# Linear attention then a GELU MLP on one Trainium2 core: counts made on VectorE and TensorE instead of GpSimd, a shorter row of idle products, and new orders for the periods

## The chip, the cores and the metric

The kernel runs on one core of a Trainium2 chip. A core has a matrix engine (TensorE; PE in the profile, its weight loads PEld), a vector engine (VectorE, DVE), an activation engine (ScalarE, ACT), a general engine (GpSimd, POOL) and SyncE (SP). Each works through its own list of instructions in order, and they wait for each other by semaphores. Sixteen DMA engines move data between device memory and the core's own memory; here POOL's queue issues all loads and converts float32 to bfloat16 on the way, and SP's queue issues the stores and some transposes. Products land in PSUM; the kernel names eight banks of it: `uY`, `uV`, `uZ`, `mY`, `mR`, `a0`, `a1`, `a2`.

The metric is the device time of one execution in microseconds (us). The kernel before has a median of 207.54 us over three runs (207.53 to 207.77).

## What is computed

Decayed linear attention over 4 sequences of 768 positions with 8 heads of 64, then an MLP with exact GELU over the 3072 resulting rows:

```python
for b in range(nb):                       # blocks of the sequence
    intra = (qb @ kb.T * Dmask) @ vb      # Dmask[i, j] = lam ** (i - j) for i >= j, else 0
    inter = (qb * lam_pow) @ kv_state
    out[:, :, sl] = intra + inter
    kv_state = lam_block * kv_state + (kb * rev_pow).T @ vb
x = out.transpose(0, 2, 1, 3).reshape(3072, 512)
h = x @ w_in                              # 512 -> 2048
y = gelu(h) @ w_out                       # 2048 -> 512, float32 out
```

The kernel takes blocks of 128 positions where the reference takes 64; the decay makes the two the same.

## The kernel before, in words

The 768 positions are cut into six groups (`NG = 6`) of 128 positions for all four sequences, that is, 512 rows a group. Group g's attention gives `xs[g]`, then the first MLP product with GELU gives `gts[g]`, then the second product gives the output rows. The stages overlap: while group g is in its first MLP product, group g-1 is in its second one and group g+1 in attention. TensorE's list is written out by hand, as strings of letters that are worked off one after the other, and the place of a letter sets the place of its instructions on every engine's list.

**The head** (`HEAD`, L727). POOL issues the loads in the order of `LOADS1`, behind the first load of k (L129) and of q (L132). `load(0, 0, ..)` is half a group, two DMAs. Between the two loads POOL writes two iotas (L130, L131): `pos`, the number of the partition, and `row`, the counts 0 to 127 along the free axis. From them VectorE makes the identity `ident` for the transposes and the thresholds `posp`, `negj` and masks `cmask_p`; ScalarE makes powers of lam (`lam_mp`, `lam_q`). In `HEAD`, "." is one idle product (`keep_warm`, L740), 128 x 512 on zeros, whose result nobody reads; K and Q are transposes of k and q (`p_transposes`, L340), S scores and their masks (`p_scores`), O attention outputs (`p_outputs`, L389, then `p_x` L404), m and n parts of the first MLP product (`mm1_part`), z state products. Two of the masks `m_p` are made by POOL (L186), between its loads.

**Groups 0 and 1** (`PHASE1`, L819; `PHASE2`, L838): p is a part of group 0's second product, i, w and t make sums of weights on VectorE (`sums_w_in`, `sums_w_out`), k, q, s, o, h are steps of attention.

**The periods** (loop at L873, g = 2 to 5). Both MLP products use Strassen's scheme in Winograd's form, seven products for eight. The first product of group g is cut into four units, each with seven products p1 to p7 (`unit_slots`, L545); one product is four matmuls of 256 columns, a *slot*. A unit works in three PSUM banks: p5 fills `uV`, which ScalarE copies to `Vs` in SBUF (L586); p1 fills `uY`; ScalarE copies `uY` over `uV` (the *seed*, L578); then p2 adds to `uV`, which becomes block X, and p6 may add to `uY`. After p6 VectorE adds `uY` and `Vs` into `uZ` (L606), after p7 into `Vs` (L615); p3 adds to `uZ`, p4 to `uY`. GELUs on ScalarE (L568) empty the four blocks, and the bank of a block can be written again after its GELU. So there are four short chains between slots: p1, seed, p6; p6, add, p7; p7, add, p4; p4, GELU, p1 of the next unit. The second product of group g-1 has 28 slots of the same size (`mm2_slots`, L632). The strings `PA` (g = 2), `PB` (3 and 4) and `PC` (5) interleave them: a is the next slot of the units (order 1 5 6 2 7 3 4 in the first unit, 5 1 6 2 7 3 4 in the others), m the next slot of the second product, v a visit of attention for group g+1 (`front` and `outputs`), h a scaling of v on ScalarE, x a sum of x on VectorE, Y a decay of the state, c a DMA transpose, K, Q, V loads. `LA`, `LB` and `LC` give lags: how many slots later an add or a mask goes on VectorE's list. Attention of the last group is done in period 4, so in period 5 its PSUM banks (`a0`, `a1`, `a2`) are free until the second product of group 5 takes `a0` and `a1`.

After the periods the second product of group 5 runs alone.

Of the kernel before, what the change touches and what calls it, by code (L numbers as in the profile page):

```python
# [8 lines left out]
F32 = mybir.dt.float32  # L9
BF16 = mybir.dt.bfloat16  # L10
ALU = mybir.AluOpType
# [4 lines left out]
def kernel(  # L16
# [11 lines left out]
    B, H, S, D = q.shape  # L28
    d_model, d_ff = moe_w_in.shape
    C = 128  # L30
    NG = S // C
# [32 lines left out]
    def later(n, fn):  # L64
        later_no[0] += 1
        later_list.append((slot_no[0] + n, later_no[0], fn))
# [21 lines left out]
    def load(g, pair, name):  # L88
        if pair == 0:
            raw[g, name] = raw_pool.tile([128, B, H, D], BF16, tag="r" + name, name="raw_" + name, bufs=1 if name == "q" else 2)  # L90
        t = raw[g, name].rearrange("p (n a) h d -> p n (a h d)", n=2)[:, pair].rearrange("p (h t d) -> p h t d", h=H, t=2)
        for b in range(2):
            G.dma_start(t[b * 64:(b + 1) * 64].rearrange("p h t d -> p h (t d)"),
                        dram[name][2 * pair + b, :, g * C:(g + 1) * C, :].rearrange("h (p t) d -> p h (t d)", t=2))
        raw[g, pair, name] = t
# [17 lines left out]
    s_in = [w_pool.tile([128, 2, d_ff // 2], BF16, name=f"s_in{i}") for i in range(4)]  # L113
# [13 lines left out]
    pos = consts.tile([128, 1], F32)  # L127
    row = consts.tile([128, C], F32)
    load(0, 0, "k")  # L129
    G.iota(pos, pattern=[[0, 1]], base=0, channel_multiplier=1, allow_small_or_imprecise_dtypes=True)  # L130
    G.iota(row, pattern=[[1, C]], base=0, channel_multiplier=0, allow_small_or_imprecise_dtypes=True)  # L131
    load(0, 0, "q")  # L132


    idle = consts.tile([128, 256], BF16)
    V.memset(idle, 0.0)  # L136
    ident = consts.tile([128, 128], BF16)
    cmask = consts.tile([128, 2, C], F32)
    cmask_p = consts.tile([128, 2, 2, 64], F32)
# [20 lines left out]
    for hi in range(2):  # L160
        p = slice(hi * D, (hi + 1) * D)
# [383 lines left out]
    def unit_slots(g, u, lags):  # L545

        x = xs[g].rearrange("p k s c -> p k (s c)")
        lo, hi = 2 * u * 128, 1024 + 2 * u * 128
        st = {}
        t = gts[g]  # L550
        bl, bh = slice(2 * u, 2 * u + 2), slice(8 + 2 * u, 10 + 2 * u)

        def prod(dst, w, f0, x_of, start):
            for b in range(2):
                for ko in range(2):
                    P.matmul(dst[:, b, :], w(ko, f0 + b * 128), x_of(ko),  # L556
                             start=(start and b == 0 and ko == 0), stop=True, skip_group_check=True)

        wl = lambda ko, f: w_in_t[:, ko, f:f + 128]
        wh = lambda ko, f: w_in_t[:, 2 + ko, f:f + 128]  # L560
        ws = lambda i: (lambda ko, f: s_in[i - 1][:, ko, f:f + 128])
        x11 = lambda ko: x[:, ko, 0:256]
        x21 = lambda ko: x[:, 2 + ko, 0:256]
        x22 = lambda ko: x[:, 2 + ko, 256:512]
        tx = lambda i: (lambda ko: t_x[g][i - 1][:, ko, :])

        def gelu(name, dst, src):
            A.activation(dst, src, ACT.Gelu)  # L568
            done.add(("g", g, u, name))
            if name in "ZW" and ("g", g, u, "Z") in done and ("g", g, u, "W") in done:  # L570
                later(lags["S"][0], lambda: sums_g(g, u, 1))
            if all(("g", g, u, n) in done for n in "XYZW"):
                for n, i in enumerate((2, 4, 3)):
                    later(lags["S"][1 + n], lambda i=i: sums_g(g, u, i))

        def seed():
            if "V" in st and "Y" in st:
                A.copy(st["V"], st["Y"])  # L578
                done.add(("seed", g, u))

        def p5():
            need(("tx", g, 1))
            st["V"] = bank("uV", [128, 2, 256])
            prod(st["V"], ws(1), lo, tx(1), True)
            st["Vs"] = work.tile([128, 2, 256], F32, tag="Vs", name="Vs")
            A.copy(st["Vs"], st["V"])  # L586
            seed()

        def p1():
            need(("x", g, 0), ("x", g, 1))  # L590
            st["Y"] = bank("uY", [128, 2, 256])
            prod(st["Y"], wl, lo, x11, True)
            seed()

        def p2():
            need(("seed", g, u))
            prod(st["V"], wh, lo, x21, False)
            gelu("X", t[:, bl, 0:256], st["V"])

        def p6():  # L600
            need(("seed", g, u), ("tx", g, 2))
            prod(st["Y"], ws(2), lo, tx(2), False)

            def z():
                st["Z"] = bank("uZ", [128, 2, 256])
                V.tensor_add(st["Z"], st["Y"], st["Vs"])  # L606
                done.add(("Z", g, u))
            later(lags["Z"], z)

        def p7():  # L610
            need(("Z", g, u), ("tx", g, 3))
            prod(st["Y"], ws(3), lo, tx(3), False)

            def w():
                V.tensor_add(st["Vs"], st["Y"], st["Vs"])  # L615
                done.add(("W", g, u))
                gelu("W", t[:, bh, 256:512], st["Vs"])
            later(lags["W"], w)

        def p3():  # L620
            need(("Z", g, u))
            prod(st["Z"], ws(4), lo, x22, False)
            gelu("Z", t[:, bl, 256:512], st["Z"])

        def p4():
            need(("W", g, u), ("tx", g, 4))
            prod(st["Y"], wh, hi, tx(4), False)
            gelu("Y", t[:, bh, 0:256], st["Y"])

        return [p5, p1, p6, p2, p7, p3, p4]  # L630

    def mm2_slots(g, lags):  # L632
# [91 lines left out]


    LOADS1 = "Q1 i0 V0 K1 m1 i4 m0 V1 i2 i1 i5 s0 i3 w0 s1 i7 i6 k0 q0 w1 w4 w2 w5 k1 q1 v0 v1 w3 w6 w7"
    HEAD = "b . . . . . . . . . . . . . K M M . . . . Q d . . . . S S Q . . . . . . . . . O . . . . K . . S . S m . . . g O m n z n n n m m m n m m n m n n"  # L727

    def script(text, actions):
        for word in text.split():  # L730
            fn = actions[word]
            (fn.pop(0) if isinstance(fn, list) else fn)()

    tags = ["uY", "uV", "uZ"]
    idle_ps = {}

    def idle_bank(tag):
        idle_ps[0] = bank(tag, [128, 2, 256], F32, "idle_ps")

    def keep_warm():  # L740
        P.matmul(idle_ps[0], idle[:, :128], idle[:, None, :].to_broadcast((128, 2, 256)), start=True, stop=True)  # L741

    part_no = [0]

    def mm1_part(g, i, pair, lag=None):
# [22 lines left out]
    for item in LOADS1.split():  # L768
        i = int(item[1:])
# [8 lines left out]
        else:  # L778
            load(int(item[0].islower()), i, item[0].lower())
    script(HEAD, {  # L780
        ".": keep_warm,
        "g": lambda: (need("lam_q"), A.activation(warm, pos, ACT.Gelu)),
        "d": decays,
        "M": [lambda x=x: mask_p(0, x, V) for x in range(2)],
        "b": lambda: idle_bank("uZ"),
        "K": [lambda i=i: p_transposes(0, i, "k", "mY", ((A, A), (V, A))[i]) for i in range(2)],
        "Q": [lambda i=i: p_transposes(0, i, "q", "mR", ((V, A), (A, A))[i]) for i in range(2)],
        "S": [lambda i=i: p_scores(0, i // 2, i % 2, (("a0", "a1"), ("uY", "uV"), ("a0", "a1"), ("mY", "mR"))[i]) for i in range(4)],
# [27 lines left out]
        "z": lambda: p_state_products(1, ("a0", "a1")),  # L816
        "y": lambda: decay(2, raw["tmp", 1]),
    }
    PHASE1 = "i i i w k q i p p p w p s k q p p p t s p p w t h s h o w p p p p s p p o p"  # L819
    script(PHASE1, attn_1)  # L820


# [12 lines left out]
    new_gs(1)  # L835
    new_x(2)
    L2S = "2393225802261242"
    PHASE2 = "q z m k y n s q m n h s k n V m K s o n m n t s h m t Q c n c o Z x c M x m m c n m x x n"  # L838

    def digits(text, i, n):  # L840
        return [int(c) for c in text[i * n:(i + 1) * n]]

    script(PHASE2, {
        "m": [lambda i=i: mm1_part(1, i, 0, L2S) for i in (0, 4, 1, 5, 2, 6, 3, 7)],
# [19 lines left out]

    PA = "mKaammmahmQvhYaaamaahYmamYhhmmaYhhhmmaavammcamVmcaacvmammmaavcaaamavmaammaxaxxmmamxm"
    PB = "hQaKahhhhvmhmhhmVamvmaamamamamammaammacvacamamamccmavamammamavamamxmaamaaxxmammx"
    PC = "aammmmamamamaammaammamaammaaamammamaaammaamammaammamamma"
    LA = "2211100002302032034341221002332000000020022"  # L870
    LB = "2010000142522221213032570306003201000104020"
    LC = "0000011000112251125020230133113202105202242"
    for g in range(2, NG):  # L873
        seqs, lag = {2: (PA, LA), 5: (PC, LC)}.get(g, (PB, LB))
        LZ, LW, LS, LM, LV = lag[0:4], lag[4:8], lag[8:24], lag[24:28], lag[28:43]
# [16 lines left out]
        for c in seqs:  # L892
# [6 lines left out]
            elif c == "v":  # L899
                i = visits.pop(0)  # L900
# [5 lines left out]
            elif c == "c":  # L906
                x = cross.pop(0)
                if g + 2 < NG:
                    crossbar(g + 2, *x)
            elif c == "h":  # L910
                h = heads.pop(0)
                if att:
                    scale_v_group(g + 1, h)
            elif c == "x":
                i = sums.pop(0)
# [41 lines left out]
```

## Time and profile before

| | |
|---|---|
| runs | 207.54 us (207.53 to 207.77), three runs |
| the profiled execution | 206.72 us, of which its span is 204.6 us |
| TensorE busy | 198.7 us, 97% of the span |
| VectorE, ScalarE, GpSimd busy | 145.7, 121.4, 71.2 us |
| idle products | 40, 12.8 us |
| moved by DMA | 23.48 MB in the packets traced |

Times inside the trace count from the start of the span. A row of the timeline gives start, duration, engine, line, operation, what it writes and reads, shape and count; behind it in brackets, the idle time of its engine before it and what ended it. A row of the chain (of work that ended last) gives start, duration, engine, tile and line, and how many instructions were merged. "Busy" of TensorE is modelled: matmuls are pipelined, so a matmul counts as busy from its issue to its modelled end, and short waits between two matmuls show not as idle time but as longer groups in the chain.

### The profile page before, as it was taken

How to read it: one execution, taken by the hardware profiler on the slowest of the kernel's cores; microseconds unless marked ns; L12 is line 12 of the kernel's file. 1: busy time of each engine (PE TensorE's matmuls, PEld its weight loads, DVE VectorE, ACT ScalarE, POOL GpSimd, SP SyncE). 2: the span in 40 equal slices, each digit the busy share in tenths (PEclk: the TensorE clock that was granted, in tenths of full speed). 3: DMA queues.
4: the chain of work that ended last, by engine and by line, in shares of the span. 5: the costliest groups of instructions: out<-in, count | busy, mean ns of one | idle time of the engine just before them, and what ended most of it. 6: DMA issues, size and time to landing. Idle time of an engine off the chain costs nothing.

```text
span 204.6 us, 6259 instructions
## 1 busy us (share of the span) xinstructions
PE 198.7 (97%) x2648; PEld 156.1 (76%) x2648; DVE 145.7 (71%) x315; ACT 121.4 (59%) x248; POOL 71.2 (35%) x97
## 2 busy tenths in 40 slices
PE   7998999999999999999999999999999999999993
PEld 2454788545578888888878888888888888888882
DVE  3477482859657899699989599797699655765243
ACT  5445466283479857973588753788555566654310
POOL 7999977866493099100077100000000000000000
PEclk9999999999999999999999999999999999999999
DMA  5999999999999999994729997230002030011214
GB/s 54 141 181 180 188 182 198 183 195 181 239 160 152 125 138 119 145 99 104 157 53 157 147 144 145 83 103 3 0 3 94 13 103 3 0 51 60 97 54 155
DMA packets 81580, 23.48 MB, mean 115 GB/s; under 512 B 69776, under 2 KB 81040, under 8 KB 81552
## 3 DMA queue, kind: packets, MB, share of 16 engines
q0 software_dynamic: 62704, 13.64, 80.1%
q1 hardware_dynamic: 18848, 9.44, 19.7%
q8 instruction: 21, 0.34, 0.7%
q14 instruction: 7, 0.06, 0.1%
HBM read 27.27 MB, written 6.29 MB: 164 GB/s over the span
## 4 chain that ended last, share of the span: by engine, by line
PE 94%; DVE 3%; ACT 1%; issue 0%
PE p_uY L556 14%; PE p_mY L718 14%; PE p_mR L718 9%; PE p_uV L556 7%; PE idle_ps L741 6%; PE p_a L718 5%; PE p_uY L755 5%; PE p_uV L755 5%; PE p_uZ L755 4%; PE p_uZ L556 3%; PE t_ps L346 3%; PE p_mY L535 2%; PE p_uY L535 2%; PE p_uZ L535 2%; PE p_uV L535 2%; PE p_a L300 2%
## 5 line engine op out<-in xcount | busy, mean ns | idle before, releaser
L718 PEld LDWEIGHTS <-g_t 128*128 128x128 bf16 x304 | 29.5, 98 | 3.7
L556 PEld LDWEIGHTS <-s_in 128*128 128x128 bf16 x256 | 24.4, 97 | 5.0 <-issue 1.6
L755 PEld LDWEIGHTS <-w_in_t 128*128 128x128 bf16 x256 | 24.2, 98 | 4.8 <-issue 1.4
L718 PEld LDWEIGHTS <-gs 128*128 128x128 bf16 x240 | 23.2, 98 | 2.9
L556 PEld LDWEIGHTS <-w_in_t 128*128 128x128 bf16 x192 | 18.5, 97 | 2.9
L568 ACT ACTIVATE g_t<-p_uV 128x512 bf16<-128x512 f32 x16 | 9.5, 596 | 18.0 <-PE p_uV L556 18.0
L556 PE MATMUL p_uY<-tx,s_in 128*128 128x256 bf16 x128 | 19.2, 272 | 0.3 <-DVE p_uZ L606 0.3
L386 DVE TENSOR_TENSOR sc_m<-p_a,m_p 128x512 bf16<-128x512 f32 x20 | 12.9, 686 | 8.1 <-PE p_a L379 8.1
L606 DVE TENSOR_TENSOR p_uZ<-p_uY,Vs 128x512 f32<-128x512 f32 x16 | 11.2, 697 | 8.7 <-PE p_uY L556 8.4
L718 PE MATMUL p_mY<-w_out_t,g_t 128*128 128x256 bf16 x128 | 16.9, 273 | 0.0
L568 ACT ACTIVATE g_t<-Vs 128x512 bf16<-128x512 f32 x16 | 10.1, 630 | 10.4 <-DVE Vs L615 10.4
L615 DVE TENSOR_TENSOR Vs<-p_uY,Vs 128x512 f32<-128x512 f32 x16 | 11.0, 688 | 5.4 <-PE p_uY L556 5.1
L741 PE MATMUL idle_ps<-idle 128*128 128x512 bf16 x40 | 12.8, 463 | 1.1 <-DVE idle L136 1.1
L505 DVE TENSOR_TENSOR gs<-g_t 128x512 bf16<-128x512 bf16 x20 | 8.4, 420 | 6.4 <-ACT g_t L568 6.3
L755 PE MATMUL p_uV<-x_t,w_in_t 128*128 128x256 bf16 x88 | 11.6, 273 | 1.2 <-DVE x_t L408 1.2
L108 POOL DMA_DIRECT2D raw_v<-in_v_dram x12 | 9.9, 859 | 7.9 <-ACT o_sb L541 4.5
L100 POOL DMA_DIRECT2D raw_q<-in_q_dram x3 | 5.2, 1736 | 20.9 <-DMA qT<-raw_q 20.9
L586 ACT COPY Vs<-p_uV 128x512 f32<-128x512 f32 x16 | 9.4, 591 | 4.0 <-PE p_uV L556 4.0
L755 PE MATMUL p_uY<-x_t,w_in_t 128*128 128x256 bf16 x88 | 11.4, 273 | 0.0
L535 PEld LDWEIGHTS <-g_t 128*128 128x128 bf16 x64 | 5.7, 97 | 6.7
L578 ACT COPY p_uV<-p_uY 128x512 f32<-128x512 f32 x16 | 9.2, 573 | 2.4 <-PE p_uY L556 2.2
L568 ACT ACTIVATE g_t<-p_uZ 128x512 bf16<-128x512 f32 x16 | 9.5, 591 | 1.8 <-PE p_uZ L556 1.8
(148 smaller groups left out, 472.8 us busy)
## 6 DMA issues: line engine op xcount, KB each, us to landing
raw_k<-in_k_dram POOLq DMA_DIRECT2D x24, 128.0 KB, 6.7
raw_v<-in_v_dram POOLq DMA_DIRECT2D x24, 128.0 KB, 6.1
w_in_t<-in_moe_w_in_dram POOLq DMA_DIRECT2D x8, 256.0 KB, 6.2
w_out_t<-in_moe_w_out_dram POOLq DMA_DIRECT2D x8, 256.0 KB, 7.1
raw_q<-in_q_dram POOLq DMA_DIRECT2D x12, 128.0 KB, 6.3
raw_q<-in_q_dram POOLq DMA_DIRECT2D x3, 512.0 KB, 9.5
out_dram<-P1s SPq DMA_DIRECT2D x5, 256.0 KB, 2.4
out_dram<-Vs SPq DMA_DIRECT2D x5, 256.0 KB, 2.5
```

The lines of the kernel that those rows point to most:

```text
L108: G.dma_start(t[slot * 64:(slot + 1) * 64, hi], dram[name][:, hi::2, g * C + half * 64:g * C + half * 64 + 64, :].rearrange("b j si d -> s ...
L386: V.tensor_mul(sc_m[g, pair][half][:, :, hi], sc[hi], m_ph[:, hi, 2 * half:2 * half + 2])
L535: P.matmul(mo[io], gts[g][:, kf, io * C:(io + 1) * C], w_out_t[:, kf, :], start=(part == 0 and j == 0), stop=(part == 3 and j == 3))
L556: P.matmul(dst[:, b, :], w(ko, f0 + b * 128), x_of(ko), start=(start and b == 0 and ko == 0), stop=True, skip_group_check=True)
L568: A.activation(dst, src, ACT.Gelu)
L578: A.copy(st["V"], st["Y"])
L586: A.copy(st["Vs"], st["V"])
L606: V.tensor_add(st["Z"], st["Y"], st["Vs"])
L615: V.tensor_add(st["Vs"], st["Y"], st["Vs"])
L718: P.matmul(st[dst][:, io, :], a(kf, io), b(kf), start=(new and u == 0 and io == 0 and kf == 0), stop=True, skip_group_check=True)
L741: P.matmul(idle_ps[0], idle[:, :128], idle[:, None, :].to_broadcast((128, 2, 256)), start=True, stop=True)
L755: P.matmul(h[:, j, :], w_in_t[:, ki, kf * 128:(kf + 1) * 128], x[:, ki, w], start=(ki == 0 and j == 0), stop=True, skip_group_check=True)
```

## The change

1. The iotas go. `row` is made by VectorE: a zero in column 0, then seven additions that double the counted stretch (1, 2, 4 up to 64 columns). Its first partition is copied as bfloat16 into `one`, a scratch row in the still unused tile `s_in[3]`; one TensorE product of that row with a 1 turns it upright in bank `a2`, and VectorE copies it to `pos`. POOL issues the load of q directly behind that of k.
2. Idle products: three before that product and 31 in `HEAD` instead of 40 in `HEAD`: 13 before the first K become 3 + 7, nine before the first O become seven, two behind the second K become one. Their helper functions move up in the file; the bank's word "b" goes.
3. In the last period the seed goes from `uY` into attention's bank `a2`, as soon as p1 is there, and p2 adds to that bank; `uV` only holds p5 until it is copied. In the other periods the seed is as before, under the name `X`.
4. `PHASE1`: the second w moves ahead of the fourth i, and one p from before "s k q" to behind it. `PHASE2`: Q and the first c move behind the o and Z that followed them.
5. New `PA`, `PB`, `PC` and lags.

```diff
     load(0, 0, "k")
-    G.iota(pos, pattern=[[0, 1]], base=0, channel_multiplier=1, allow_small_or_imprecise_dtypes=True)
-    G.iota(row, pattern=[[1, C]], base=0, channel_multiplier=0, allow_small_or_imprecise_dtypes=True)
     load(0, 0, "q")
 
 
     idle = consts.tile([128, 256], BF16)
     V.memset(idle, 0.0)
+
+    one = s_in[3][0:1, 1, 0:130]
+    V.memset(row[:, 0:1], 0.0)
+    for n in (1, 2, 4, 8, 16, 32, 64):
+        V.tensor_scalar(row[:, n:2 * n], row[:, 0:n], float(n), None, op0=ALU.add)
+    V.memset(one[:, 128:130], 1.0)
+    V.tensor_copy(one[:, 0:128], row[0:1])
+    idle_ps = {}
...
+    def keep_warm():
+        P.matmul(idle_ps[0], idle[:, :128], idle[:, None, :].to_broadcast((128, 2, 256)), start=True, stop=True)
+
+    idle_bank("uZ")
+    for _ in range(3):
+        keep_warm()
+    pos_ps = bank("a2", [128, 1])
+    P.matmul(pos_ps, one[:, 0:128], one[:, 128:129], start=True, stop=True)
+    V.tensor_copy(pos, pos_ps)
...
         def seed():
-            if "V" in st and "Y" in st:
-                A.copy(st["V"], st["Y"])
+            if g == NG - 1 and "Y" in st and "X" not in st:
+
+                st["X"] = bank("a2", [128, 2, 256])
+                A.copy(st["X"], st["Y"])
+                done.add(("seed", g, u))
+            elif "V" in st and "Y" in st and "X" not in st:
+                st["X"] = st["V"]
+                A.copy(st["X"], st["Y"])
                 done.add(("seed", g, u))
...
             need(("seed", g, u))
-            prod(st["V"], wh, lo, x21, False)
-            gelu("X", t[:, bl, 0:256], st["V"])
+            prod(st["X"], wh, lo, x21, False)
+            gelu("X", t[:, bl, 0:256], st["X"])
...
-    HEAD = "b . . . . . . . . . . . . . K M M . . . . Q d . . . . S S Q . . . . . . . . . O . . . . K . . S . S m . . . g O m n z n n n m m m n m m n m n n"
+    HEAD = ". . . . . . . K M M . . . . Q d . . . . S S Q . . . . . . . O . . . . K . S . S m . . . g O m n z n n n m m m n m m n m n n"
...
-    PHASE1 = "i i i w k q i p p p w p s k q p p p t s p p w t h s h o w p p p p s p p o p"
+    PHASE1 = "i i i w k q w i p p p s k q p p p p t s p p w t h s h o w p p p p s p p o p"
...
-    PHASE2 = "q z m k y n s q m n h s k n V m K s o n m n t s h m t Q c n c o Z x c M x m m c n m x x n"
+    PHASE2 = "q z m k y n s q m n h s k n V m K s o n m n t s h m t n c o Z Q c x c M x m m c n m x x n"
...
-    PA = "mKaammmahmQvhYaaamaahYmamYhhmmaYhhhmmaavammcamVmcaacvmammmaavcaaamavmaammaxaxxmmamxm"
-    PB = "hQaKahhhhvmhmhhmVamvmaamamamamammaammacvacamamamccmavamammamavamamxmaamaaxxmammx"
-    PC = "aammmmamamamaammaammamaammaaamammamaaammaamammaamammamma"
-    LA = "2211100002302032034341221002332000000020022"
-    LB = "2010000142522221213032570306003201000104020"
-    LC = "0000011000112251125020230133113202105202242"
+    PA = "mKaammmahmQvYhaaYamaahmaYmhhhmmaYhhmmaavammcamVmcaacvmammmaavcaaamavmaammaxamxxmamxm"
+    PB = "hQKaahhhhhvmhmhmVamvaaammamamammmaammacvcaaammamccmavaamammmavamamxmaamaaxxmammx"
+    PC = "aammmaammamamaammammamamaamamaammamaaammamaammaammmaamma"
+    LA = "2211100012302032034341422002332000020000022"
+    LB = "2011000142412241113032570106003201000104120"
+    LC = "0002011010112251123222230133043201105002144"
```

More of the change, by code (lines that the diff above doesn't have):

```diff
@@ L136, with idle_bank @@
     V.memset(idle, 0.0)
+    one = s_in[3][0:1, 1, 0:130]
[5 more added lines that the diff above has]
+    idle_ps = {}
+    def idle_bank(tag):
+        idle_ps[0] = bank(tag, [128, 2, 256], F32, "idle_ps")
+    def keep_warm():
[6 more added lines that the diff above has]
+    V.tensor_copy(pos, pos_ps)
     ident = consts.tile([128, 128], BF16)
@@ L734 @@
     tags = ["uY", "uV", "uZ"]
[L735 to L741, printed above, removed]
     part_no = [0]
@@ L784 @@
         "M": [lambda x=x: mask_p(0, x, V) for x in range(2)],
-        "b": lambda: idle_bank("uZ"),
         "K": [lambda i=i: p_transposes(0, i, "k", "mY", ((A, A), (V, A))[i]) for i in range(2)],
@@ L863 @@
     flush()
-    PA = "mKaammmahmQvhYaaamaahYmamYhhmmaYhhhmmaavammcamVmcaacvmammmaavcaaamavmaammaxaxxmmamxm"
-    PB = "hQaKahhhhvmhmhhmVamvmaamamamamammaammacvacamamamccmavamammamavamamxmaamaaxxmammx"
-    PC = "aammmmamamamaammaammamaammaaamammamaaammaamammaammamamma"
-    LA = "2211100002302032034341221002332000000020022"
-    LB = "2010000142522221213032570306003201000104020"
-    LC = "0000011000112251125020230133113202105202242"
+    PA = "mKaammmahmQvYhaaYamaahmaYmhhhmmaYhhmmaavammcamVmcaacvmammmaavcaaamavmaammaxamxxmamxm"
+    PB = "hQKaahhhhhvmhmhmVamvaaammamamammmaammacvcaaammamccmavaamammmavamamxmaamaaxxmammx"
+    PC = "aammmaammamamaammammamamaamamaammamaaammamaammaammmaamma"
+    LA = "2211100012302032034341422002332020000020022"
+    LB = "2011000142412241113032570106003201000104120"
+    LC = "0002011010112251123222230133043201105002144"
     for g in range(2, NG):
```

## The prediction, made before the changed kernel was run

> **What bounds the kernel now.** I read the page first (share of each engine, then the chain that ended last), then TensorE's waits, then the timeline of the first 24 us, then the chain through the periods.
>
> ```profile
> PE 198.7 (97%) x2648; PEld 156.1 (76%) x2648; DVE 145.7 (71%) x315; ACT 121.4 (59%) x248; POOL 71.2 (35%) x97
> PE 94%; DVE 3%; ACT 1%; issue 0%
> PE p_uV L755 <- DVE x_t L408: 1.2, 1, 1.2
> ```
>
> The first two lines are of the page: 97% and 94% mean that nearly everything is TensorE's list played off. The third is the longest wait that the view of waits finds for it. So the change can only shorten TensorE's list (idle products), or take out short waits that hide inside the chain's groups.
>
> The head is different: 40 idle products stand there because operands are not there yet. Its timeline:
>
> ```profile
> 1.07 5.73 PE L741 MATMUL idle_ps<-idle 128*128 128x512 bf16 x13 [1.07 <-DVE idle L136]
> 1.27 1.48 POOL L93 DMA_DIRECT2D raw_k<-in_k_dram  x2 [0.81 <-POOLq L941]
> 3.10 2.74 POOL L93 DMA_DIRECT2D raw_q<-in_q_dram  x4
> 11.11 1.08 POOL L186 TENSOR_TENSOR m_p<-cmask_p,lam_mp 128x512 f32<-128x512 f32 x1
> 12.83 0.68 DVE L386 TENSOR_TENSOR sc_m<-p_uV,m_p 128x512 bf16<-128x512 f32 x1
> 13.16 0.24 PE L400 MATMUL p_a<-sc_m,raw_v 64*64 64x128 bf16 x1
> 13.36 0.24 PE L400 MATMUL p_mR<-sc_m,raw_v 64*64 64x128 bf16 x2
> ```
>
> POOL issues its loads without a pause. The next fence has the issue of three loads and, for each, the time from issue to landing: the second half of v, of the second k, of the second q.
>
> ```profile
> 7.25 0.73 POOL L93 DMA_DIRECT2D raw_v<-in_v_dram  x1
> DMA to landing us min/median/max: 6.1/6.1/6.1
> ...
> 8.59 0.75 POOL L93 DMA_DIRECT2D raw_k<-in_k_dram  x1
> DMA to landing us min/median/max: 6.2/6.2/6.2
> ...
> 5.14 0.71 POOL L93 DMA_DIRECT2D raw_q<-in_q_dram  x1
> DMA to landing us min/median/max: 5.3/5.3/5.3
> ```
>
> They land at 7.25 + 6.1 = 13.35, 14.8 and 10.4. The first O's product that reads v's second half runs at 13.36, 0.2 behind its neighbour: it waited for that landing. The scores' last mask ends at 12.83 + 0.68 = 13.51, and it came late because POOL's mask (11.11 + 1.08 = 12.19) stands in POOL's list behind the loads. The second K starts at 14.96 (below), 0.15 after its landing. So in the head POOL's list and the loads are the bound, and the idle products fill what is left.
>
> **The change, part by part.**
>
> *Iotas out.* k's issue ends at 1.27 + 1.48 = 2.75, q's begins at 3.10: the two iotas hold POOL for 0.35. Every later load and POOL mask moves up by that. Do landings follow? Two windows of the stage view (length, then busy time by engine, granted clock, DMA share, GB/s):
>
> ```profile
> 4.00:6.00 2.00, 2.00 (x6) 0.76 (x5) 1.44 (x8) 1.43 (x4) 2.00 (x4) 1.00 1.22 115
> 6.00:8.00 2.00, 2.00 (x21) 0.83 (x20) 0.57 (x1) 0.54 (x2) 2.00 (x4) 1.00 1.63 156
> ```
>
> Between 4 and 6 us the DMA engines moved 115 GB/s, against 156 just after: room for 2 x (1 - 115/156) = 0.5 us of transfer. So an earlier q finds free engines, and the 0.35 can go through to the landings. I take 0.33; the ends are 0 (the queue sets the landings whatever POOL does) and, were the loads no bound at all, the idle products (below).
>
> *The new chain for `pos`.* Small VectorE operations of the same kind:
>
> ```profile
> 3.22 0.29 DVE L144 TENSOR_SCALAR ident<-row,pos 128x128 bf16<-128x128 f32 x1 [2.21 <-POOL row L131]
> 3.42 0.15 DVE L145 TENSOR_SCALAR posp<-pos 128x1 f32<-128x1 f32 x1
> 3.60 0.21 DVE L146 TENSOR_SCALAR posp<-posp,pos 128x1 f32<-128x1 f32 x1
> ```
>
> A dependent one follows after 0.18. A memset behind that of `idle` (about 1.06), seven doublings at 0.18 to 0.25 (1.35 to 1.5), a copy of one row (0.2): `one` is there at 2.7. The product (estimate 0.2 to 0.3, from these small steps) and the copy out (0.2) give `pos` at about 3.2, where VectorE now waits until 3.22 (2.21 idle). It costs nothing: K, which wants `ident` first, isn't reached before 5.9 (next part). That cover lasts for a chain up to 2 us longer; beyond, K and all behind it would wait.
>
> *TensorE.* Three idle products at 5.73/13 = 0.44 end at 2.4; it waits for `one` until 2.75, then the small product, seven idle products until 2.95 + 7 x 0.43 = 5.95. K then runs 0.85 sooner than before. From here the chain's own rows:
>
> ```profile
> 6.80 0.62 PE t_ps L346 x15
> 7.41 0.97 PE idle_ps L741 x4
> 11.19 2.05 PE idle_ps L741 x9
> 13.99 0.97 PE idle_ps L741 x4
> 14.96 0.63 PE t_ps L346 x16
> 19.56 1.35 DVE x_t L408 x2
> ```
>
> K, four idle products, Q, four more, S S: they meet the second q, which lands at 10.4 - 0.33 = 10.1. Its transposes (0.62) end at 10.75; seven idle products (0.23 each) end at 12.35. There O finds v at 13.35 - 0.33 = 13.0 and the last mask at 13.2: TensorE waits 0.6, and O ends at 13.65 instead of 13.99. K follows after four idle products at 14.6 (landing 14.5); the idle product taken out behind it was hidden by kT's copy. Then k, scores, masks, O, `x_t` (19.56) and the next part at 20.9 hang on each other and shift as one. So six idle products out (3 x 0.44 + 3 x 0.24 = 2.0) give only **-0.33**. Were nothing late, it would be 2.0 less the wait for `one` and the small product (0.5): -1.5, the other end.
>
> *PHASE1, PHASE2.* The same slots in the same groups; one p of four products moves past "s k q".
>
> ```profile
> 31.55 0.68 POOL L93 DMA_DIRECT2D raw_q<-in_q_dram  x1
> DMA to landing us min/median/max: 7.5/7.5/7.5
> ...
> 39.77 1.01 PE t_ps L346 x32
> ```
>
> Its k and q transposes (39.77, q in the second half, 40.3) come one p (0.9) and 0.33 sooner, q at 39.1; q landed at 31.55 + 7.5 = 39.05, and its load moves up by up to 0.33 too. VectorE's earlier w is behind the copies of the first k and q, and nothing of TensorE waits for it in these slots. **0**; 0.1 if the load stays.
>
> *Periods.* A slot without a wait takes 0.44. The chain shows those that waited (the first row is one that did not); two rows are ScalarE's:
>
> ```profile
> 116.61 0.44 PE p_uV L556 x4
> 114.75 0.61 ACT L586 COPY Vs<-p_uV 128x512 f32<-128x512 f32 x1
> 115.39 0.57 ACT L578 COPY p_uV<-p_uY 128x512 f32<-128x512 f32 x1
> 116.03 0.58 PE p_uY L556 x4
> 145.37 0.58 PE p_uY L556 x4
> 102.05 0.62 DVE p_uZ L606
> 169.79 0.50 PE p_uY L556 x4
> 172.91 0.58 PE p_uY L556 x4
> 174.37 0.58 PE p_uY L556 x4
> ```
>
> I set the letters beside the groups. 116.03 and 145.37 are p6 of unit 1 in periods 3 and 4, two slots after p1: ScalarE's list has the seed (115.39 to 115.96) behind a copy that started only at 114.75. New `PB` has three slots between p1 and p6: **-0.14 each, -0.28**. Two slots between p6 and p7 of unit 3 stay, and so does period 2's p7 behind the two state adds (102.05).
>
> In period 5, 169.79 (p4, two slots after p7: now three) goes, -0.06; 174.37 (p7, two after p6: now three) goes, -0.14; 172.91 (p6: its seed stood behind a Vs copy; p5 now lies two slots before p1) goes, -0.14; unit 2's p7, two slots after its p6, stays. New: unit 1's p4 only two slots after p7, +0.06. In units 2 and 3 p5 now stands right before p1, so seed and Vs copy meet on ScalarE; as the seed no longer writes the bank that the copy reads, they follow at list pace: 0 to 0.13 each, I take 0.02. Sum **-0.24**, ends -0.34 and +0.02.
>
> Sum: -0.33 - 0.28 - 0.24 = **-0.85**. The profiled execution took 206.72, 0.82 below the median; I apply the sum to the median: 207.54 - 0.85 = 206.7.
>
> **Rivals.**
> 1. *The DMA queue sets the landings* and the 0.35 vanishes in it. For it: time to landing grows from 5.3 to 6.2. Against: the room at 4 to 6 us. Time 207.54 - 0.52 = 207.0.
> 2. *The idle products come out in full*, since no landing binds: -1.5 - 0.52, 205.5. Against: 13.35 beside 13.36.
> 3. *The new orders give nothing*, because lists on ScalarE or VectorE come out differently: head alone, 207.2.
> 4. *TensorE stays slow in the head* (slower side). Idle products took 0.44 each up to 6.80, 0.24 from 7.41: the rate changed after 5.7 us of unbroken products. Now there is a gap of about 0.4 at 2.4, then only 3.0 us of idle products, then transposes. If the slow rate holds up to O, work of 13.99 - 6.80 - 0.46 = 6.7 takes 0.44/0.24 = 1.8 times as long, 12.1, so O ends at 18.0 instead of 13.65: 206.7 + 4.4 = 211.1. It decides (over 0.4 slower than before) if the fast rate comes after about 11 us: 0.45 of the time since 6.8 is lost, 0.6 of it in O's wait. For it: the stretch 1.07 to 6.8 was enough, and nothing shows that less is. [...]
> 5. *New waits in the periods* (slower side). In `PB` p7 of units 0 and 2 now comes right behind p2 and a visit; if its add stands behind the visit's masks, each p7 waits as that of 102.05 did: there the add ended at 102.66 and its slot ran 0.49 late. Four such, 206.7 + 1.96 = 208.7; it decides from three on.
>
> ```profile
> 109.10 0.70 DVE L606 TENSOR_TENSOR p_uZ<-p_uY,Vs 128x512 f32<-128x512 f32 x1
> ```
>
> Against: this add (unit 0, period 3) ended at 109.80. Unit 0's p7 stands eleven slots before 116.03, at 111.2, and one sooner in the new order: 110.8, a full 1.0 later, and the add's lag is the same.
>
> **How the numbers follow.** Forecast 0.50 (own range 206.2 to 207.1); rivals 1: 0.13, 2: 0.06, 3: 0.12, 4: 0.11, 5: 0.08. A change under 0.2%, 0.4 us, can't be told from none. Forecast, 1 and 2 are faster: 0.69; 3 is the same: 0.12; 4 and 5 slower: 0.19. The range 205.9 to 208.0 takes in the forecast, 1 and 3, and leaves out 2, most of 4 and 5.
>
> **What would show it.** q's first issue at 2.75; v's second half landing near 13.0 and the part behind `x_t` at 20.6 instead of 20.9; p6 of unit 1 without 0.58 in periods 3 and 4; about 0.3 in period 5. The prediction is wrong if idle products behind K still take 0.44, if landings stay where they were, or if new groups over 0.44 stand in front of p7.

## The result and the profile after

The changed kernel took 206.05 us (median of four runs, 205.87 to 206.17) beside 207.53 for the kernel before on the same chip: ratio 0.9942, 95% interval 0.9920 to 0.9965. Measured a second time it took 206.11 beside 207.25, ratio 0.9955 (0.9936 to 0.9973). It is faster by about half a per cent; 206.7 had been forecast. (The ratios here and below are not the quotients of the two medians, so the two need not agree.) The two profiled executions stand at 206.72 before and 205.87 after, their spans at 204.6 and 203.7 (204.61 and 203.75 in the trace, 0.86 apart).

The page of the changed kernel, with TensorE's share and the make-up of the chain that ended last:

```profile
PE 196.5 (96%) x2643; PEld 155.4 (76%) x2643; DVE 147.2 (72%) x326; ACT 120.7 (59%) x248; POOL 71.0 (35%) x95
...
PE 88%; DVE 4%; DMA 3%; POOL 3%; issue 1%; ACT 1%; POOLq 0%
```

TensorE has 2.2 us less to do, yet the span shrank by 0.85. The rest became waiting: the chain now has POOL and a load in it, which it did not have before. The view of TensorE's waits says which:

```profile
PE p_uV L772 <- DVE x_t L427: 1.2, 1, 1.2
...
PE p_a L154 <- DVE s_in L141: 0.6, 1, 0.6
PE t_ps L365 <- DMA raw_q<-in_q_dram: 0.4, 1, 0.4
...
PE p_mR L419 <- DMA raw_v<-in_v_dram: 0.2, 1, 0.2
```

The first is the old one, unchanged. The second is the wait for `one`. The third is a load that idle products covered before. The last, for v, was there before too (0.20 between O's first two rows, 13.16 and 13.36), but hidden in a group's modelled busy time. Rows of the head's timeline:

```profile
1.28 1.48 POOL L93 DMA_DIRECT2D raw_k<-in_k_dram  x2 [0.82 <-POOLq L957]
...
2.75 2.73 POOL L93 DMA_DIRECT2D raw_q<-in_q_dram  x4
3.09 0.18 PE L154 MATMUL p_a<-s_in 1*128 1x1 bf16 x1 [0.56 <-DVE s_in L141]
3.21 3.06 PE L148 MATMUL idle_ps<-idle 128*128 128x512 bf16 x7
3.50 0.29 DVE L163 TENSOR_SCALAR ident<-row,pos 128x128 bf16<-128x128 f32 x1
6.20 0.64 PE L365 MATMUL t_ps<-ident,raw_k 128*64 128x128 bf16 x16
8.23 0.64 PE L365 MATMUL t_ps<-ident,raw_q 128*64 128x128 bf16 x16 [0.43 <-DMA raw_q<-in_q_dram]
12.98 0.24 PE L419 MATMUL p_mR<-sc_m,raw_v 64*64 64x128 bf16 x2 [0.20 <-DMA raw_v<-in_v_dram]
14.64 0.64 PE L365 MATMUL t_ps<-ident,raw_k 128*64 128x128 bf16 x16
```

POOL issues q directly behind k, at 2.75 instead of 3.10. The second K starts at 14.64 instead of 14.95, and what hangs on it shifts as one.

The chain, first in the head, then in the periods:

```profile
6.88 6.05 DMA raw_v<-in_v_dram
...
94.99 0.52 PE p_uY L575 x4
...
102.42 0.60 PE p_uY L575 x4
...
115.74 0.44 PE p_uY L575 x4
...
131.97 0.58 PE p_uY L575 x4
...
144.94 0.44 PE p_uY L575 x4
...
165.72 0.44 PE p_uY L575 x4
...
175.32 0.51 PE p_uY L575 x4
...
179.36 0.58 PE p_uY L575 x4
```

The first row is the load that the chain goes through now: v's second half, issued at 6.88, landed at 12.94. 115.74 and 144.94 are p6 of unit 1 in periods 3 and 4: the 0.58 is gone in both. What remains is p7 (94.99 in unit 2 and 102.42 in unit 3 of period 2; 131.97 in unit 3 of period 3; 179.36 in unit 2 of period 5) and p4 of unit 1 in period 5 (175.32).

From the start of one period's first slot to the next, and from the last to the end of the units, in us:

| | period 2 | 3 | 4 | 5 | sum |
|---|---|---|---|---|---|
| before | 29.28 | 29.35 | 28.84 | 25.15 | 112.62 |
| after | 29.41 | 29.21 | 28.69 | 24.88 | 112.19 |
| difference | +0.13 | -0.14 | -0.15 | -0.27 | -0.43 |

Ahead of them the part behind `x_t` starts 0.32 sooner (20.64), and the stretch from group 0's second product (35.48) to the periods (76.06) is 0.10 shorter: 0.32 + 0.10 + 0.43 = 0.85. Behind the units both kernels take 15.5. Of these parts the 0.10 is not the change's: `idles_only` and `iotas_only` (below), with `PHASE1` and `PHASE2` as before, have the shorter stretch too (40.58, where the kernel before has 40.68).

One run below needs a word: in the profiled execution of `best_orders` the granted clock fell to half from 15.60 to 19.01 us and it took 208.71, so its trace is used only for landings before that and from the periods on, and its time is the median of its three other executions.

### The profile page after: what moved, and what is told of

Its sections match the earlier page's. It is cut to its first block, busy times and chain, and to the rows that moved or that the text cites. A ratio compares the mean times of both kernels' runs of the same rounds, so it can differ in the third digit from the quotient of the medians.

```text
span 203.7 us, 6258 instructions
## 1 busy us (share of the span) xinstructions
PE 196.5 (96%) x2643; PEld 155.4 (76%) x2643; DVE 147.2 (72%) x326; ACT 120.7 (59%) x248; POOL 71.0 (35%) x95
## 3 DMA queue, kind: packets, MB, share of 16 engines
q1 hardware_dynamic: 18848, 9.44, 19.6%
## 4 chain that ended last, share of the span: by engine, by line
PE 88%; DVE 4%; DMA 3%; POOL 3%; issue 1%; ACT 1%; POOLq 0%
PE p_mY L743 14%; PE p_uY L575 14%; PE p_mR L743 9%; PE p_uV L575 6%; PE p_a L743 5%; PE p_uY L772 5%; PE p_uV L772 5%; PE p_uZ L772 4%; PE p_uZ L575 3%; DMA raw_v<-in_v_dram 3%; PE t_ps L365 2%; PE p_uZ L554 2%; PE p_uY L554 2%; PE p_mY L554 2%; PE p_uV L554 2%; PE p_a L319 2%
## 5 line engine op out<-in xcount | busy, mean ns | idle before, releaser
L587 ACT ACTIVATE g_t<-p_uV 128x512 bf16<-128x512 f32 x12 | 7.1, 594 | 13.5 <-PE p_uV L575 13.5
L148 PE MATMUL idle_ps<-idle 128*128 128x512 bf16 x34 | 10.9, 451 | 1.1 <-DVE row L137 1.1
L256 ACT ACTIVATE vs<-raw_v,lam_m 128x256 bf16<-128x256 bf16 x24 | 10.6, 504 | 0.0
```

Source lines behind the costliest of these rows:

```text
L256: A.activation(vs[g][:, :, h, :], raw[g, "v"][:, :, h, :], ACT.Copy, scale=lam_m[:, h:h + 1])
```

## The experiments

The theory: POOL's earlier loads and the free slots ahead of p6 and p7 make the gain; TensorE's own list in the head (the idle products) does not bind. The rivals: the idle products themselves bind; the clock comes late; the DMA queue sets the landings; the orders give nothing. Every batch ran beside the kernel before on one chip (its medians: 207.07, 207.31, 207.25); of these batches only the third has the changed kernel itself, so the first two batches are compared with the kernel before.

**The two halves of the change.** `head_only` is the changed kernel with the strings and the seed of before (`PC` and `LC` stand here for all of them):

```diff
...
-    PC = "aammmaammamamaammammamamaamamaammamaaammamaammaammmaamma"
+    PC = "aammmmamamamaammaammamaammaaamammamaaammaamammaammamamma"
-    LC = "0002011010112251123222230133043201105002144"
+    LC = "0000011000112251125020230133113202105202242"
...
```

> The head of the change alone (no iotas, 34 idle products), strings and seed of before. Theory of the prediction: the group of products behind x_t starts 0.32 sooner than before, and nothing else moves, so the span is 0.3 shorter and the runs about 0.35 us shorter (ratio 0.998). Rival, since the runs gained 1.5 where the two traces differ by 0.85: the rest lies in the head, and this kernel gains about 0.9 in the runs (ratio 0.9955).

206.67 beside 207.07, ratio 0.9978 (0.9957 to 0.9999). In its trace the part behind `x_t` started at 20.86, only 0.10 sooner than before, since v's second half landed at 13.13. Its span was long (205.4) through a wait of 0.92 at 66.5 us, of which below.

`periods_only` is the reverse: the kernel before with the strings and seed of after.

> New orders of PHASE1, PHASE2, the periods and the seed of the last period; the head as before. Theory of the prediction: period 5 ends 0.5 to 0.55 sooner than before, runs about 0.5 us shorter (ratio 0.9975). Rival (the head holds more of it): the same 0.5 here, but less than half of the whole. Rival (new orders give nothing): 0.

206.92 beside 207.07, ratio 0.9986 (0.9964 to 1.0008). By the clock alone that could be nothing. The trace is far sharper: its periods took 29.39, 29.20, 28.70 and 24.87, sum 112.16 beside 112.62, 0.46 less.

Period 2 needs a second look, since the changed kernel's was 0.13 longer. With the old orders it took 29.28 in the kernel before, but 29.36 in `head_only`, `iotas_only` and `idles_only`; with the new ones, 29.38 to 29.42. Much of that is p7 of unit 0: here in the kernel before, in `head_only` with the same orders, and in the changed kernel:

```profile
80.71 0.44 PE p_uY L556 x4
...
81.43 0.53 PE p_uY L575 x4
...
80.30 0.53 PE p_uY L575 x4
```

So this wait of 0.10 comes and goes whatever the orders (`cold`, with the new ones, lacks it). Only the wait of 0.07 at p7 of unit 2 (94.99 above) belongs to the new orders: every trace with them has it, and none of the four with the old ones. Beside the three other traces of the old orders (sum 112.67 to 112.68) the new ones are worth about 0.5, as expected, whatever the head does. The third rival, that they give nothing, falls.

**What binds in the head.** `iotas_only` is `head_only` with as many idle products as before, 3 and 10 ahead of K, nine ahead of O:

```diff
-    HEAD = ". . . . . . . K M M . . . . Q d . . . . S S Q . . . . . . . O . . . . K . S . S m . . . g O m n z n n n m m m n m m n m n n"
+    HEAD = ". . . . . . . . . . K M M . . . . Q d . . . . S S Q . . . . . . . . . O . . . . K . . S . S m . . . g O m n z n n n m m m n m m n m n n"
```

> No iotas, but 40 idle products as before (3 ahead of the product for the counts, 10 behind it). Theory: landings come 0.3 sooner as in the change, but TensorE's list now is longer by the wait for the counts and the small product (0.86 in the changed kernel's trace), so O ends near 14.8 instead of 13.99 and the kernel is 0.8 us slower than before (ratio 1.004). Rival (POOL's 0.35 counts by itself): 0.3 faster.

206.97 beside 207.07, ratio 0.9983 (0.9964 to 1.0003). Its timeline:

```profile
3.20 4.43 PE L148 MATMUL idle_ps<-idle 128*128 128x512 bf16 x10
7.56 0.64 PE L365 MATMUL t_ps<-ident,raw_k 128*64 128x128 bf16 x16
13.83 0.24 PE L419 MATMUL p_a<-sc_m,raw_v 64*64 64x128 bf16 x1
```

K came 0.83 later than before (6.73), and the first O product 0.87 after v's second half was there (12.96). But the first state products, at the end of the head, started at 23.11 beside 22.68: 0.43 later, not 0.8. The kernel before had itself been waiting, 0.20 at O for v and most of the rest for the second q, so half of the longer list fell into waits that were there already. The clock does not show even that: its interval ends at 1.0003. Beside `head_only`, the six idle products more cost 0.52 in the traces (state products at 23.11 beside 22.59) and 0.30 between the medians, whose intervals overlap. So with the iotas gone the old list would bind, by the trace; the two halves of the head's change need each other.

`idles_only` is the other piece: the idle products of after, the iotas of before.

```diff
-    HEAD = "b . . . . . . . . . . . . . K M M . . . . Q d . . . . S S Q . . . . . . . . . O . . . . K . . S . S m . . . g O m n z n n n m m m n m m n m n n"
+    HEAD = "b . . . . . . . . . . K M M . . . . Q d . . . . S S Q . . . . . . . O . . . . K . S . S m . . . g O m n z n n n m m m n m m n m n n"
```

> Idle products cut to 34 as in the change (10, 7 and 1 in place of 13, 9 and 2), iotas stay. Theory: the landing of v's second half (13.3) and of the second k (14.8) hold TensorE, O still ends at 14.0, the same time as before within 0.1 us (ratio 1.000). Rival (the idle products count in full): 2.0 us faster (ratio 0.990).

207.31 beside 207.07, ratio 1.0005 (0.9979 to 1.0031). Its timeline:

```profile
5.64 0.64 PE L346 MATMUL t_ps<-ident,raw_k 128*64 128x128 bf16 x16 [0.71 <-DMA raw_k<-in_k_dram]
7.87 0.64 PE L346 MATMUL t_ps<-ident,raw_q 128*64 128x128 bf16 x16 [0.63 <-DMA raw_q<-in_q_dram]
13.13 0.24 PE L400 MATMUL p_mR<-sc_m,raw_v 64*64 64x128 bf16 x2 [0.26 <-DMA raw_v<-in_v_dram]
```

Six idle products less, K 1.1 sooner, and nothing of it left at O: each went into a wait for k, q and v, and the state products started at 22.62 beside 22.68. This refutes the second rival, that the idle products come out in full: with the iotas in place these six were filler.

`cold` leaves out every idle product ahead of K:

```diff
-    for _ in range(3):
-        keep_warm()
...
-    HEAD = ". . . . . . . K M M . . . . Q d . . . . S S Q . . . . . . . O . . . . K . S . S m . . . g O m n z n n n m m m n m m n m n n"
+    HEAD = "K M M . . . . Q d . . . . S S Q . . . . . . . O . . . . K . S . S m . . . g O m n z n n n m m m n m m n m n n"
```

> The changed kernel without the ten idle products ahead of the first K (24 left). It tells what they are worth. Theory A (the rate of TensorE comes from unbroken work before): transposes and idle products run at 0.44 a product until several us after K, O ends after 13.6; if the fast rate comes only after 11 us, the kernel is over 0.5 us slower than the changed one, up to 4. Theory B (landings hide it): K waits for its load at 5.5 anyway, O still waits for v at 13.0, and the time is that of the changed kernel within 0.2 us.

206.85 beside 207.31, ratio 0.9991 (0.9977 to 1.0006). Its timeline:

```profile
5.56 1.06 PE L363 MATMUL t_ps<-ident,raw_k 128*64 128x128 bf16 x16 [2.30 <-DMA raw_k<-in_k_dram]
6.55 1.89 PE L148 MATMUL idle_ps<-idle 128*128 128x512 bf16 x4
8.87 0.89 PE L363 MATMUL t_ps<-ident,raw_q 128*64 128x128 bf16 x16 [0.43 <-DMA raw_q<-in_q_dram]
9.69 1.04 PE L148 MATMUL idle_ps<-idle 128*128 128x512 bf16 x4
```

Four idle products took 1.89, then 1.04: full clock was granted at 9.44, 3.9 us after the first transpose. (That is the start of the trace's first clock record; the view of windows prints 1.00 ahead of it too.) In the nine other traces with the changed head it was granted between 5.06 and 7.69, in the kernel before at 6.87. So the slow TensorE of the fourth rival is there in this trace, and this is its price: K and four idle products 1.3 us longer, Q at 8.87 instead of 8.23. O still waited for v, but only because v landed at 14.32 in this run. TensorE reached O at 13.78, 0.21 of that through a wait for a late second q; in `head_only` v's second half was there and in use at 13.18. With landings as in `head_only` the late clock would have cost 0.4 to 0.6 (an estimate from these rows). The times can't settle it: `better_all`, run beside it with the idle products and as long in the periods (112.24 beside 112.16), took 206.58, and the intervals overlap. So theory B is not shown. In the nine it came 4.0 to 6.6 us after the first idle product, which starts at 1.07.

**The landings.** In ten of the 14 traces the head's end follows one number, whichever head they have. "v" is the landing of v's second half, "state" the start of the first state products:

| run | iotas | v | state | difference |
|---|---|---|---|---|
| before | yes | 13.31 | 22.68 | 9.37 |
| periods_only | yes | 13.71 | 23.02 | 9.31 |
| idles_only | yes | 13.09 | 22.62 | 9.53 |
| after | no | 12.94 | 22.36 | 9.42 |
| after_again | no | 13.14 | 22.51 | 9.37 |
| head_only | no | 13.13 | 22.59 | 9.46 |
| better_all | no | 13.14 | 22.59 | 9.45 |
| old_seed | no | 13.30 | 22.70 | 9.40 |
| better_pa | no | 13.86 | 23.18 | 9.32 |
| cold | no | 14.32 | 23.78 | 9.46 |

The difference stays within 0.22 while v moves by 1.4. So v's landing bounds the head in these ten. In the other four something else comes last: TensorE's list in `iotas_only` (10.15), q in `loads_first` and `best_all` (10.86 and 10.89, below), and the half clock in `best_orders` (10.42). The landing of one and the same head (the six rows from `after` to `better_pa`) runs from 12.94 to 13.86, and to 14.49 with `best_orders`, which has that head too; with the iotas it runs from 13.09 to 13.71. The medians of the rows, 13.14 and 13.31, are 0.17 apart, well inside that spread.

**The seed of period 5.** `old_seed` has the new order with the seed as it was:

```diff
-            if g == NG - 1 and "Y" in st and "X" not in st:
-                st["X"] = bank("a2", [128, 2, 256])
...
+            if "V" in st and "Y" in st:
+                A.copy(st["V"], st["Y"])
```

> The changed kernel with the old seed (over uV) in the last period, orders as changed. Theory: the seed there again waits for the copy of uV; p6 of units 0, 2 and 3, whose p5 stands right beside p1, wait about 0.13 each, period 5 ends 0.3 to 0.4 later than in the changed kernel (ratio to it 1.0015 to 1.002). Rival (the orders alone did it): the same as the changed kernel.

207.02 beside 207.31, ratio 0.9986 (0.9963 to 1.0010). Period 5 took 25.21 beside 24.88: 0.33 more, and 0.06 more than with the old order and the old seed. The chain shows where; p6 of unit 0 and of unit 2 (0.13 and 0.08 of it; the other 0.12 is at p6 of unit 3):

```profile
166.56 0.56 PE p_uY L575 x4
...
179.02 0.53 PE p_uY L575 x4
```

In the changed kernel the first of these is 165.72 above, 0.44. The new `PC` puts p5 closer to p1 and needs the seed out of `uV`: without that it is worth nothing. The new seed with the old `PC` was not tried.

**Better orders.** `better_pa` puts the adds of period 2 a slot sooner, against the 0.60 at 102.42:

```diff
-    LA = "2211100012302032034341422002332020000020022"
+    LA = "1210100012302032034341422002332020000020022"
```

> The changed kernel with two lags of period 2 changed: the add before p7 of units 0 and 3 goes one slot sooner on VectorE's list (LA begins 1210 instead of 2211), so in unit 3 it stands ahead of the two state adds. Theory: the group of 0.59 at p7 of unit 3 in period 2 (0.48 over a free one) goes, and at unit 0 0.1 more: 0.5 us faster than the changed kernel. Rival: the state adds or the add after p7 come late instead, and the wait moves to p4 or to the next period: no gain.

207.04 beside 207.31, ratio 0.9989 (0.9972 to 1.0006), and period 2 took 29.96, 0.55 longer. The rival was right: the wait moved to the next period. ScalarE's timeline, then the chain:

```profile
103.64 1.71 ACT L354 ACTIVATE state<-tmp,lam_c 128x256 bf16<-128x256 f32 x4 [0.90 <-DVE tmp L346]
105.26 0.61 ACT L587 ACTIVATE g_t<-Vs 128x512 bf16<-128x512 f32 x1
105.78 0.57 ACT L587 ACTIVATE g_t<-p_uZ 128x512 bf16<-128x512 f32 x1
106.25 0.58 ACT L587 ACTIVATE g_t<-p_uY 128x512 bf16<-128x512 f32 x1
```

```profile
106.25 0.59 ACT g_t L587
106.84 0.04 issue
106.88 0.60 PE p_uY L575 x4
```

The add for p7 went ahead of the state's additions, so the four decays on ScalarE came later and stood for 1.71 in front of three GELUs; the next period's first product waited 0.90 for the last of them.

`better_all` has that and new orders for periods 3 to 5:

```diff
-    PB = "hQKaahhhhhvmhmhmVamvaaammamamammmaammacvcaaammamccmavaamammmavamamxmaamaaxxmammx"
+    PB = "hQKaahhhhhvmhmhmVamvaaammamamammmaammacvcaaammamccmavaamammavaammmxaammaaxxmammx"
-    PC = "aammmaammamamaammammamamaamamaammamaaammamaammaammmaamma"
+    PC = "aammaammamamaammammamamaammamaammamamaammamaammaammaamma"
```

> As better_pa, and one m slot moved in PB from before p4 of unit 2 to behind p1 of unit 3, and a PC in which p6 to p7 and p7 to p4 have three slots between wherever the 28 m slots allow. Theory, counted in waits of the chain: 0.15 less in each of periods 3 and 4, 0.2 less in period 5, so 0.5 us on top of better_pa, 1.0 us faster than the changed kernel. Rival: lists on VectorE and ScalarE shift and new waits of 0.1 to 0.5 eat it.

206.58 beside 207.31, ratio 0.9975 (0.9946 to 1.0004). Periods 3, 4 and 5 took 29.05, 28.54 and 24.66: 0.16, 0.15 and 0.22 less than after, as expected; period 2 took 29.99 again, so that nothing is left in the sum (112.24 beside 112.19).

**Once more, and three further versions.** These four ran together.

> The changed kernel once more, with nothing altered. If what the change is worth is what the two traces show (0.85 us of span, 0.4%), its median stands 0.7 to 1.0 us below that of the kernel before, ratio 0.995 to 0.9965. If the 1.48 us between the first two medians was right and the trace missed some of it, the ratio is 0.993 again. If landings that vary from run to run made up most of the first difference, it is nearer 0.998.

206.11 beside 207.25, ratio 0.9955 (0.9936 to 0.9973): 1.14 us, between the trace's 0.85 and the first 1.48; the ratio lies where the first of the three expectations put it. Its profiled execution took 207.01, and its chain shows 0.34 of "issue" that the changed kernel's first trace hasn't got (the stretch from group 0's second product to the periods is 0.52 longer):

```profile
64.95 0.76 PE p_uV L772 x6
65.71 0.34 issue
66.06 0.39 PE p_uV L772 x2
```

`loads_first` moves loads only:

```diff
-    LOADS1 = "Q1 i0 V0 K1 m1 i4 m0 V1 i2 i1 i5 s0 i3 w0 s1 i7 i6 k0 q0 w1 w4 w2 w5 k1 q1 v0 v1 w3 w6 w7"
+    LOADS1 = "Q1 V0 K1 i0 m1 m0 V1 i4 i2 i1 i5 s0 i3 w0 s1 i7 i6 k0 q0 w1 w4 w2 w5 k1 q1 v0 v1 w3 w6 w7"
```

> The changed kernel with three of GpSimd's load issues in another order: v's second slice, k's second slice and one mask come ahead of the first slice of w_in, which needs them later. If the DMA queue's landings set the head (the first rival's rule, and the reading that the 0.20 wait for raw_v and the late second half of v are the bound), the second half of v lands about 0.7 us earlier (12.2 in place of 12.94), the last output product of head 0 ends near 13.2 in place of 13.69, and the span is about 0.4 us shorter. If TensorE's own order sets it, v lands earlier and the part behind x_t still starts at 20.6, nothing gained. A third outcome: w_in, now later, is late for the first products of MLP layer 1, which lose 0.3 us or more there.

206.02 beside 207.25, ratio 0.9945 (0.9923 to 0.9968), nothing beyond the changed kernel. v landed at 11.26, 1.7 sooner, and the part behind `x_t` started at 20.40, only 0.24 sooner: the wait went over to q's first half. Timeline and chain:

```profile
8.48 0.64 PE L365 MATMUL t_ps<-ident,raw_q 128*64 128x128 bf16 x16 [1.03 <-DMA raw_q<-in_q_dram]
...
8.96 2.15 POOL L205 TENSOR_TENSOR m_p<-cmask_p,lam_mp 128x512 f32<-128x512 f32 x2
```

```profile
32.25 7.64 DMA raw_q<-in_q_dram
39.89 0.04 issue
39.94 0.64 PE t_ps L365 x16
```

Both masks now stand side by side on POOL, which issues no load for 2.15 us; later loads land about 1.5 us later: POOL's waits for two loads of w_out end at 35.89 and 37.35 instead of 34.34 and 35.91, and a later q arrives at 39.89 instead of 38.3, for which TensorE waits 0.86. What the head gained was given back, and more, 20 us on. That the two masks caused all of the delay was not tried.

`best_orders` takes the orders of `better_all` and, for period 2, moves the state's last additions instead of the add:

```diff
-    LA = "2211100012302032034341422002332020000020022"
+    LA = "2211100012302032034341422002332020000020300"
```

> The changed kernel with period 2 issuing the last state adds at once (the last three digits of LA 022 become 300, x_t one step behind them) and with the orders of periods 3 to 5 in which the two units of the largest waits at p7 are moved apart. Where the order alone sets the waits: period 2 loses its 0.48 wait at the last unit's p7 and the four state decays on ScalarE come early enough that no GELU stands behind them, about 0.3 us; periods 3 and 4 give 0.15 each and period 5 0.22, as in the run with both better orders; 0.8 us together against the changed kernel, a span near 202.9. If the state decays land before a GELU again, period 2 loses 0.5 as in the two runs before it and the sum is about 0.

204.68 beside 207.25, ratio 0.9876 (0.9856 to 0.9897). Periods 2 to 5 took 28.92, 29.05, 28.55 and 24.65: 1.02 less than after, where 0.8 was expected; period 2 gave 0.49 instead of 0.3. The chain at p7 of unit 3, in periods 2 and 3:

```profile
104.63 0.44 PE p_uY L575 x4
...
134.02 0.44 PE p_uY L575 x4
```

They were 0.60 and 0.58. The decays came in time and no GELU was late. `best_all` has the edits of `loads_first` and of `best_orders`.

> Both of the preceding edits. They lie in different stages, so by the theory that each stage is bound by its own last wait they add: 0.4 us in the head and 0.8 us in the periods, a span near 202.5 and a ratio to the kernel before near 0.990. If the head's gain is given back by the wait for the last mask or for w_in in the stages behind it, the ratio is that of the run with the orders alone.

205.27 beside 207.25, ratio 0.9906 (0.9881 to 0.9932). The periods are those of `best_orders` within 0.02 (sum 111.16); the loads bring the late q again (0.93 at 39.58). Of all kernels tried, `best_orders` has the lowest time, from three executions; its interval and that of the last overlap.

## Why the prediction was right

- **The sum** was -0.85 for the profiled executions and came out at -0.86. That it fits so closely is partly luck: 0.10 of it is not the change's, period 2 of the kernel before was 0.08 short of its other traces, and the landing varies (next point).
- **The time** was put at 206.7, from the median of the kernel before; it came out at 206.05 and 206.11, near the low end of the range. The medians gained 1.48 and 1.14. Whether there is a gain beyond 0.85 is open: 0.85 is a ratio of 0.9959, inside both intervals. The pair of traces shows two short executions (only 12 of 87 later ones of the kernel before took less than 206.72, none of 13 of the changed kernel less than 205.87), and no pair shows what the longer ones lose.
- **Iotas, -0.33**: -0.32 in the pair of traces, through the landing of v that was named (forecast 13.0, measured 12.94). The landings of other runs make that agreement partly luck: by the medians only 0.17 would be due to the change. `head_only` gained 0.4 by the clock, with an interval from 0.0 to 0.9. So the first rival, that the queue swallows the 0.35, is not excluded for the half of it.
- **The chain for `pos`, 0**: right in cost, short in time. `one` was there at 3.03, not 2.7, `ident` at 3.50 instead of 3.22; K at 6.20 hid it.
- **TensorE's list**: here single steps failed and the end did not. K came at 6.20, not 5.95. Then Q waited 0.43 for q's first half; only the second half had been looked up. Both were absorbed by the wait at O. That six of them only fill is shown by `idles_only`, for the head with iotas; without the iotas they no longer do (`iotas_only`).
- **PHASE1, PHASE2, 0**: the stretch is 0.10 shorter, because one group at 71 took 0.57 instead of 0.67. It took 0.57 in `idles_only` too, with the strings of before, so the change did not do it.
- **PB, -0.28**: -0.29, both at p6 of unit 1, and the p7 of unit 3 stayed as said.
- **PC, -0.24**: -0.27, slot by slot as listed: three waits gone, p4 of unit 1 at 0.51, unit 2's p7 at 0.58. `old_seed` shows that with the old seed 0.33 is lost again.
- **Period 2, nothing**: it became 0.13 longer in the pair of traces, mostly by waits of 0.10 at p7 of unit 0 and 0.07 at p7 of unit 2. The first comes and goes with the old orders too; the second is the new orders' own. The prediction had weighed new waits at p7 only for `PB`. Which of the new letters and digits makes it was not tried.
- **The slow TensorE** (rival 4) did not come: nine traces with the changed head were at full clock by 7.69. `cold` shows what it would have been: with no idle products ahead of K the clock came at 9.44, 0.4 to 0.6 worth by the estimate above, far from the rival's 4.4. **New waits in the periods** (rival 5) came in period 2 instead of `PB`, one of 0.07 where the rival had 0.49 each.

## What to carry to other kernels

Before idle products or an engine's list are shortened, look what lands last behind them: here O waited for a load, and six idle products less only gave longer waits (`idles_only`: the state products at 22.62 beside 22.68). Read a gain of less than one per cent stage by stage from the traces, where periods 3 to 5 repeat within 0.02 us, and give a landing seen once the spread of the same load in other traces (0.9 us here). The cause of a wait at a slot can be two lists away: in period 2 moving what goes ahead of it (the state's additions) gave 0.49, moving the waiting add itself cost 0.55.

## What was not expected of the hardware

- **One load's landing varies by 0.9 us** between six executions of the same head whose issues agree within 0.02: v's second half, issued at 6.86 to 6.88, landed at 12.94 to 13.86. With `cold` (14.32) and `best_orders` (14.49), issued at the same time, it is 1.6.
- **A wait at 66 us comes and goes.** Four of 14 traces have 0.3 to 0.9 there, in the middle of eight equal products, with no releaser ("issue"). The trace has transfers of 16 KB on a queue named "instruction", one every 4 to 8 us in this stretch. In the four traces with the wait, the one due there ended at 64.36 (wait 0.52), 64.52 (0.53), 64.61 (0.32) and 64.90 (0.92); in eight of the others it ended at 63.64 or sooner; the other two, `cold` and `best_orders`, ran this stretch one to two us later than the rest. That TensorE got its list too late there is a guess of the author's; no run tried it.
- **Full clock was granted 3.1 to 6.6 us after the first product**, over 13 traces that begin with idle products at 1.07. From the soonest to the latest it is 3.5 us. What sets the moment was not shown.
